# Taking part of the exponential off ScalarE: one score tile of six, in three of seven steps, computed by GpSimd and VectorE

## The chip, the cores and the metric

The kernel runs on one core of a Trainium2 chip. The metric is the device time of one execution in microseconds (us). Before the change it is 322.8 us (322.55 to 322.87 in the runs taken beside the changed kernel). All runs compared below are fast unless a run is called slow, which here means that it took over 1.5% longer than the fastest of its kernel. In the profiles, PE is TensorE's matmul, PEld its weight load, ACT ScalarE, DVE VectorE, POOL GpSimd, SP SyncE; "L280" is a line of that run's own source, so the same statement has another number before and after: the tanh is L271 before and L280 (in two runs L282) after, the exp L275 and L284, the scores' matmul L262 and L271, the pass of pv L292 and L322 (L321).

## The reference

Attention with a tanh soft cap, then a soft mixture of experts on its result. Only the first half matters here:

```python
scores = scale * np.matmul(q, k.transpose(0, 1, 3, 2))   # 8 batches, 12 heads, 448 x 448, head size 64
scores = cap * np.tanh(scores / cap)                      # cap = 30
attn = np.exp(scores - scores.max(-1, keepdims=True))
attn = attn / (attn.sum(-1, keepdims=True) + 1e-09)
x = np.matmul(attn, v)                                    # then x goes through _moe_ref(x, phi, w1, w2)
```

q and k are drawn with a deviation of 0.1, so the scores lie near 0. The kernel leaves the maximum out.

## The kernel before

A "step" handles one chunk j of six score tiles of 128 x 448 elements. ScalarE applies two tanh (three tiles each, out of PSUM) and one exp (six tiles, in SBUF). TensorE makes the scores of the next chunk and multiplies the chunk before by V (a pass of pv); VectorE normalises pv, casts k and q, and copies transposes. Seven steps make a period, one small exp of router logits (E) ends it.

```python
def tanh_chunk(i):
    j, half = divmod(i, CH // CS)                # CH = 6 tiles a chunk, CS = 3 tiles a tanh
    if half == 0:
        exs[j] = exps.tile([P, CH, S], BF16, name="ex", tag="ex")      # a ring of four
    ...
        act.activation(exs[j][:, half * CS + u0:half * CS + u1, :],
                       sc[:, u0:u1, 0:S], ACT.Tanh, scale=qk_scale / cap)

def exp_part(j, u0, u1):
    act.activation(exs[j][:, u0:u1, :], exs[j][:, u0:u1, :], ACT.Exp, scale=cap)

for j in range(NCH):                             # NCH = 56 steps (simplified: first and last ones cut)
    run(j, "0")
    tanh_chunk(2 * j)
    tanh_chunk(2 * j + 1)
    exp_chunk(j - 1)                             # exp_part(j - 1, 0, CH)
    pv_pass(pr, 0)                               # matmuls of a pass, then VectorE's normalisation
    run(j, "a")                                  # run(): casts, transposes, logits placed in the slot
    qk_chunk(2 * j + 2)
    run(j, "b")
    pv_pass(pr, 1)
    run(j, "c")
    qk_chunk(2 * j + 3)
    run(j, "d")
...
for n, job in enumerate(wjobs):                  # loads of the experts' weights
    at(2 + n * (NCH - 6) // len(wjobs), "b", *job)
```

Everything is issued in this order, in the timelines each engine runs its instructions in it (TensorE's weight loads apart; in the changed kernel VectorE stands for GpSimd ahead of L306 in 14 of 21 cases, 17.1 us in all, and nothing behind it goes first), and pv and the transposes have one PSUM buffer each.

The softmax here doesn't subtract the row's maximum and nothing guards it: scores larger than these inputs give would overflow.

Of the kernel before, what the change touches and what calls it, by code (L numbers as in the profile page):

```python
# [1 line left out]

# [5 lines left out]

F32 = mybir.dt.float32
BF16 = mybir.dt.bfloat16  # L10
ALU = mybir.AluOpType
ACT = mybir.ActivationFunctionType
PSUM = bass.MemoryType.PSUM

P = 128
# [3 lines left out]
S = 448  # L19
CH = 6  # L20
# [2 lines left out]
GOFF = (0, 128, 256, 320)  # L23
VW = 2 * (DH + 1)
MASKED = -30000.0


@with_exitstack
def kernel(
# [14 lines left out]
    E = moe_w1.shape[0]  # L44
# [5 lines left out]
    cap = float(cap)  # L50
# [4 lines left out]
    NPAIR = 2 * NQ  # L55
    NTILE = NPAIR * NT
    NCH = NTILE // CH
    R2 = 28

    ctx.enter_context(tc.manual_schedule())  # L60
    pe, dve, act, pool, sp = nc.tensor, nc.vector, nc.scalar, nc.gpsimd, nc.sync
# [5 lines left out]

    ones = consts.tile([P, P], BF16, name="ones")
    dve.memset(ones, 1.0)
    ident = consts.tile([P, P], BF16, name="ident")  # L70
    make_identity(nc, ident)
    ones32 = consts.tile([P, 1], BF16, name="ones32")
    pool.memset(ones32, 0.0)
    pool.memset(ones32[0:NS, :], 1.0)
    mask = consts.tile([P, NG, NS], F32, name="mask")
    pool.memset(mask, 0.0)
    pool.memset(mask[0:HP, NG - 1, :], MASKED)
    phib = consts.tile([P, NJ, NS], BF16, name="phib")
    ET4 = consts.tile([P, B // 2 - 1, NT, 2, HP], BF16, name="ET4")
    winv = consts.tile([P, B // 2, NT], F32, name="winv")  # L80
    slT = consts.tile([P, NJ, NS], BF16, name="slT")
    zacc = consts.tile([P, 1], F32, name="zacc")
# [4 lines left out]
           for e in range(E - 1)]  # L87
    w2b = wts.tile([P, R2, D], BF16, name="w2b")

# [17 lines left out]
    def load_half(dst, n0, half):  # L107
# [4 lines left out]
    wjobs = [(load_w1, e, jh, fh) for e in range(E) for jh in range(2) for fh in range(2)]  # L112
    wjobs += [(load_half, w2b[:, n0:n0 + 4, half * HD:(half + 1) * HD], n0, half)
              for n0 in range(0, R2, 4) for half in range(2)]

    dram = ctx.enter_context(tc.tile_pool(name="dram", bufs=1, space=bass.MemoryType.DRAM))
    w2d = []
    for n0 in range(R2, len(blocks), 4):
        t = dram.tile([P, 2, 4, HD], BF16, name=f"w2d{n0}")
        for half in range(2):  # L120
            wjobs.append((load_half, t[:, half, :, :], n0, half))
        w2d.append(t)

    att = ExitStack()
# [5 lines left out]
    exps = att.enter_context(tc.tile_pool(name="exps", bufs=4))  # L130
    vb.append(att.enter_context(tc.tile_pool(name="vb1", bufs=1)))
    xs = att.enter_context(tc.tile_pool(name="xs", bufs=4))
    attp = ExitStack()
    psS = attp.enter_context(tc.tile_pool(name="psS", bufs=2, space=PSUM))
    psV = attp.enter_context(tc.tile_pool(name="psV", bufs=1, space=PSUM))
# [115 lines left out]
    scores, exs, pvs, xq, xTs, lgs = {}, {}, {}, {}, {}, {}  # L251

    def qk_chunk(i):
        sc = psS.tile([P, CS, 512], F32, name="sc", tag="sc")
        scores[i] = sc
        for u in range(CS):
            pr, c = divmod(i * CS + u, NT)
            Q, h = divmod(pr, 2)
            r = slice(h * HP, h * HP + HP)
            for n in range(2):  # L260
                cs = slice(n * HP, n * HP + HP)
                pe.matmul(sc[cs, u, 0:S], qkT["k", Q][r, c, cs],  # L262
                          qkT["q", Q][r, :, cs], start=True, stop=True)

    def tanh_chunk(i):
        j, half = divmod(i, CH // CS)
        if half == 0:
            exs[j] = exps.tile([P, CH, S], BF16, name="ex", tag="ex")
        sc = scores.pop(i)
        for u0, u1 in ((0, 1), (1, CS)) if i == 0 else ((0, CS),):  # L270
# [4 lines that stand above are left out]
        act.activation(exs[j][:, u0:u1, :], exs[j][:, u0:u1, :], ACT.Exp, scale=cap)  # L275

    def exp_chunk(j):
        exp_part(j, 0, CH)

    def pv_tiles(pr, half, c0, c1, home=None):  # L280

# [16 lines left out]
    def norm(pr, half):  # L298
# [7 lines left out]
            pv[:, :, :, 0:DH],  # L306
            rec.to_broadcast([P, 2, 2, DH]), op=ALU.mult)

    def pv_pass(pr, half, home=None):
        pv_tiles(pr, half, 0, NT, home)  # L310
        norm(pr, half)
# [11 lines left out]
    def logits(Q, ps=None):  # L323
# [8 lines left out]
        if hq == 0:  # L332
            lgs[b] = xs.tile([P, NG, NS], F32, name="lg", tag="lg", bufs=2)
        dve.tensor_tensor(lgs[b], ps, mask if hq == 0 else lgs[b], op=ALU.add)  # L334

# [13 lines left out]
    def e_norm(b):  # L349
# [6 lines left out]
        else:  # L356
            dve.tensor_tensor(zacc, ps, zacc, op=ALU.add)
        if b == B - 1:
# [27 lines left out]
    def slot_sums(b):  # L386
# [4 lines left out]
        else:  # L391
            dve.tensor_tensor(slacc, ps, slacc, op=ALU.add)  # L392
        for hq in range(NQB):
# [8 lines left out]
    def at(j, slot, f, *a):  # L402
        if j < 0:
            j, slot = 0, "b"
        aux.setdefault((j, slot), []).append((f, a))
# [8 lines left out]
    def quad_in(Q, cast_k, cast_q, k_in, q_in, v_in):  # L414
        if 0 < Q < NQ:
            at(*cast_k, cast, "k", Q)
            at(*cast_q, cast, "q", Q)
            at(*k_in, transp, "k", Q)
            at(*q_in, transp, "q", Q)
            at(*v_in, vcast, Q)  # L420

    for b in range(B):
        j = b * PER
        if b == 0:
            quad_in(1, (0, "a"), (0, "b"), (0, "d"), (1, "a"), (2, "d"))
        else:
            quad_in(3 * b + 1, (j - 1, "b"), (j, "a"), (j - 1, "d"), (j, "c"), (j + 1, "d"))
        quad_in(3 * b + 2, (j + 1, "c"), (j + 2, "c"), (j + 2, "b"), (j + 2, "d"),
                (j + 4, "d"))
        quad_in(3 * b + 3, (j + 4, "a"), (j + 5, "a"), (j + 4, "d"), (j + 5, "c"),  # L430
                (j + 6, "d"))
        p = 6 * b
        at(j + 1, "d", spare, 26 if b == 0 else 10)
        at(j + 2, "d" if b == 0 else "a", spare, 14)
        at(j + 2, "d" if b == 0 else "c", spare, 8)
        at(j + 3, "d", spare, 10)
        at(j + 4, "a", x_transp, p)
        at(j + 5, "a", x_transp, p + 1)
        at(j + 6, "a", x_transp, p + 2)
        at(j + 5, "d", logits, 3 * b)  # L440
        if b < B - 1:
            at(j + 7, "a", x_transp, p + 3)
            at(j + 8, "a", x_transp, p + 4)
            at(j + 7, "d", logits, 3 * b + 1)
            at(j + 9, "a", x_transp, p + 5)
            at(j + 9, "d", logits, 3 * b + 2)
            at(j + 11, "0", e_exp, b)
            at(j + 11, "d", slot_sums, b)
            if b < B - 2:
                at(j + 12, "d", e_transp, b)  # L450
            if b < B - 2:
                at(j + 13, "d", e_norm, b)
            if b % 2:
                at(j + 14, "d", e_sums, b // 2)
    for n, job in enumerate(wjobs):
        at(2 + n * (NCH - 6) // len(wjobs), "b", *job)
    for j, slot, n in ((0, "a", 10), (0, "c", 10), (1, "b", 10), (1, "c", 8)):
        at(j, slot, spare, n)
    for j, slot, n in ((NCH - 6, "d", 8), (NCH - 4, "d", 8), (NCH - 2, "d", 12)):
# [5 lines left out]
    def run(j, slot):  # L465
        for f, a in aux.pop((j, slot), []):
            f(*a)
# [20 lines left out]
    def pair_at(j):  # L488

        pr = (j + 1) * CH // NT - 1  # L490
        return pr if pr >= 0 and (pr + 1) * NT > j * CH else None

    for j in range(NCH):
        run(j, "0")
        tanh_chunk(2 * j)
        if j == NCH - 1:
            exp_chunk(j - 1)
        tanh_chunk(2 * j + 1)
        if j < 2:
            exp_chunk(j)  # L500
        elif 2 < j < NCH - 1:
            exp_chunk(j - 1)
        pr = pair_at(j - 2)
        if pr is not None:
            pv_pass(pr, 0)
        run(j, "a")
        if j == NCH - 1:
            pv_pass(pr, 1)
            busy(8, psT.tile([P, P], F32, name="filler", tag="T"))
            e_norm(B - 2)  # L510
            busy(6, psT.tile([P, P], F32, name="filler", tag="T"))
            break
        qk_chunk(2 * j + 2)
        run(j, "b")
        if pr is not None:
            pv_pass(pr, 1)
        run(j, "c")
        qk_chunk(2 * j + 3)
        run(j, "d")
    assert not aux, aux.keys()  # L520
# [44 lines left out]
    for s, gs in enumerate(halves):  # L565
        hs = slice(2 * s, 2 * s + 2)
        ps = bank([P, 2, NS], name="lpl")
        for g in gs:
# [3 lines left out]
                      start=False, stop=True)  # L572
        dve.tensor_tensor(lg[:, hs, :], ps, lg[:, hs, :], op=ALU.add)
        act.activation(el[:, hs, :], lg[:, hs, :], ACT.Exp)
# [3 lines left out]
    for s in range(2):  # L578
        js = slice(3 * s, 3 * s + 3)
        dve.tensor_tensor(slT[:, js, :], sl_ps[:, js, :], slacc[:, js, :], op=ALU.add)  # L580
    e_rep(bl)
# [9 lines left out]
    for half in range(2):  # L591
        for n0 in range(R2, len(blocks), 4):
            t = tl.tile([P, 4, HD], BF16, name=f"w2t{n0}_{half}")
            sp.dma_start(out=t, in_=w2d[(n0 - R2) // 4][:, half, :, :])
            w2t[n0, half] = t
# [3 lines left out]
    def w2_half(n, half):  # L599
        if n < R2:  # L600
            return w2b[:, n, half * HD:(half + 1) * HD]
        return w2t[n - n % 4, half][:, n % 4, :]
# [90 lines left out]
    for n in range(B // 2 * NT):  # L693
        bb, c = divmod(n, NT)
# [61 lines left out]
```

## Time and profile before

| | before |
|---|---|
| time, us | 322.8 |
| span of the profiled run, us | 321.0 |
| mean granted TensorE clock | 0.983 |
| busy, us: ScalarE / TensorE / VectorE / GpSimd | 284.4 / 273.3 / 168.6 / 104.5 |
| from one E to the next (seven steps), us | 32.92 |

The last row is (255.78 - 58.23) / 6 from the starts of E in ScalarE's timeline. The lines that carry this page, and the timeline of one group of steps, are in the prediction. One more view: the busy windows of the kernel before for three steps, with the columns start:end, length, busy us (and instruction count) of PE, PEld, DVE, ACT and POOL, granted clock, DMA share and GB/s.

```profile
77.13:81.80 4.67, 4.51 (x69) 3.30 (x67) 2.84 (x7) 4.67 (x4) 1.10 (x2) 1.00 1.16 230
81.80:86.48 4.68, 3.55 (x52) 2.44 (x50) 2.03 (x5) 4.68 (x5) 3.28 (x4) 1.00 0.77 216
86.48:91.15 4.67, 4.16 (x57) 3.04 (x57) 1.84 (x5) 4.67 (x4) 0.00 (x0) 1.00 1.15 216
```

ScalarE is busy the whole of each step, TensorE at 76 to 97% of it (3.55/4.68 to 4.51/4.67), and the clock is full. Of TensorE's 12.22 us in these three steps, 3.0 are junk matmuls, which are issued whether it is late or not.

### The profile page before, as it was taken

The page shows a single profiled execution, that of the slowest core. Times are in us where ns is not written, and L with a number is a line of the kernel's source. Part 1 is how long each engine was busy: PE and PEld are TensorE (multiplying, and loading weights), DVE is VectorE, ACT ScalarE, POOL GpSimd, SP SyncE. Part 2 cuts the span into 40 slices and gives each one's busy share as a digit, 9 for nine tenths or more (in the row PEclk, how much of TensorE's full clock was granted, in tenths as well). Part 3 has the DMA queues.
Part 4 walks back from the last instruction along what each step waited for, and adds up shares of the span by engine and source line. Part 5 has one row for each costly group of instructions (what it writes and reads, how often), then busy time and mean ns, then how long its engine had stood idle before and what let it go on. Part 6 is the DMA issues. An engine that isn't in the chain of part 4 may idle for free.

```text
span 321.0 us, 8842 instructions
## 1 busy us (share of the span) xinstructions
PE 273.3 (85%) x3827; PEld 193.6 (60%) x3827; DVE 168.6 (53%) x427; ACT 284.4 (89%) x208; POOL 104.5 (33%) x133
## 2 busy tenths in 40 slices
PE   8889988899889988898889988988889998998720
PEld 6666666666656666665666656766666667652300
DVE  3545664465546654665466546644665434327740
ACT  4998999999999999999999999999999999226730
POOL 2063525433533452445154515451643030200000
PEclk9999999999999999999999999999999999999985
DMA  8689999999999989999999999999999816678996
GB/s 240 226 178 228 225 274 238 220 229 261 220 209 251 254 197 233 238 279 240 200 231 266 227 227 218 265 225 224 224 258 201 207 51 208 225 308 307 378 414 278
DMA packets 57623, 76.91 MB, mean 240 GB/s; under 512 B 3824, under 2 KB 54128, under 8 KB 57584
## 3 DMA queue, kind: packets, MB, share of 16 engines
q0 software_dynamic: 30480, 25.22, 52.0%
q1 hardware_dynamic: 26816, 50.90, 46.5%
q8 instruction: 30, 0.49, 0.6%
q10 hardware_dynamic: 288, 0.23, 0.2%
q14 instruction: 9, 0.07, 0.1%
HBM read 90.54 MB, written 18.09 MB: 338 GB/s over the span
## 4 chain that ended last, share of the span: by engine, by line
ACT 77%; PE 13%; DVE 2%; DMA 2%; issue 2%; DVEq 0%; SPq 0%; ACTq 0%
ACT ex L271 38%; ACT ex L275 37%; PE so_ps L638 2%; PE hp L612 2%; DMA out_dram<-ob 2%; PE pv L292 1%; PE op L664 1%; PE boot L476 1%; PE junk L476 1%; PE sc L262 1%; DMA out_dram<-obh 1%; PE ps L189 1%; ACT ob L716 1%; DVE obh L666 1%; DVE xq L303 1%
## 5 line engine op out<-in xcount | busy, mean ns | idle before, releaser
L271 ACT ACTIVATE ex<-sc 128x1344 bf16<-128x1344 f32 (+1 forms) x113 | 162.4, 1693 | 2.3 <-PE pv L292 1.4
L275 ACT ACTIVATE ex<-ex 128x2688 bf16<-128x2688 bf16 (+1 forms) x57 | 161.9, 2858 | 0.1
L292 PE MATMUL pv<-vbd,ex 128*128 128x130 bf16 x1288 | 90.3, 220 | 2.1 <-ACT ex L275 0.7
L292 PEld LDWEIGHTS <-ex 128*128 128x128 bf16 x1344 | 78.8, 97 | 21.0 <-DVE xq L303 14.7
L262 PE MATMUL sc<-qT,kT 64*64 64x448 bf16 x672 | 78.7, 358 | 10.7 <-ACT ex L271 10.2
L240 POOL CAST vbd<-vraw 64x896 bf16<-64x896 f32 x23 | 21.6, 941 | 106.6 <-PE pv L292 76.2
L302 DVE RECIPROCAL rec<-pv 128x4 f32<-128x4 f32 x92 | 16.8, 183 | 60.4 <-PE pv L292 60.4
L262 PEld LDWEIGHTS <-kT 64*64 64x64 bf16 x672 | 28.0, 105 | 27.8 <-issue 10.0
L303 DVE TENSOR_TENSOR xq<-pv,rec 128x256 bf16<-128x256 f32 x92 | 39.0, 424 | 3.2
L476 PEld LDWEIGHTS <-ones 128*128 128x128 bf16 x497 | 30.4, 101 | 12.4 <-DVE xq L303 8.6
L476 PE MATMUL junk<-ones 128*128 128x128 bf16 x454 | 33.0, 219 | 2.8 <-DVE xq L303 1.9
L346 POOL COPY e<-E 128x512 bf16<-128x512 bf16 x9 | 5.5, 608 | 85.2 <-ACT E L340 49.6
L232 DVE COPY kT<-kps 128x896 bf16<-128x896 bf16 x23 | 14.4, 625 | 28.0 <-PE kps L230 28.0
L105 POOL DMA_DIRECT2D w1b<-in_moe_w_dram x32 | 24.8, 779 | 0.0
L241 POOL CAST vbd<-vraw 64x896 bf16<-64x896 f32 x23 | 23.6, 1027 | 1.3
L320 DVE COPY xT<-xps 128x512 bf16<-128x512 bf16 x47 | 19.5, 415 | 3.2 <-PE xps L318 3.2
L318 PE MATMUL xps<-ident,xq 128*128 128x128 bf16 x188 | 18.1, 218 | 0.0
L219 DVE CAST kbf<-kraw 128x896 bf16<-128x896 f32 x22 | 16.9, 767 | 0.8 <-DMA kraw<-in_k_dram 0.8
L232 DVE COPY qT<-qps 128x896 bf16<-128x896 bf16 x23 | 14.2, 618 | 4.5 <-PE qps L230 4.5
L230 PE MATMUL kps<-ident,kbf 128*128 128x128 bf16 x161 | 12.8, 219 | 4.2 <-DVE slacc L392 2.2
L230 PE MATMUL qps<-ident,qbf 128*128 128x128 bf16 x161 | 12.8, 219 | 3.2 <-DVE lg L334 2.7
L230 PEld LDWEIGHTS <-kbf 128*128 128x128 bf16 x161 | 10.0, 97 | 9.0 <-issue 8.3
(103 smaller groups left out, 229.5 us busy)
## 6 DMA issues: line engine op xcount, KB each, us to landing
w1b<-in_moe_w_dram POOLq DMA_DIRECT2D x32, 384.0 KB, 9.0
vraw<-in_v_dram SPq DMA_DIRECT2D x23, 448.0 KB, 5.3
qraw<-in_q_dram SPq DMA_DIRECT2D x22, 448.0 KB, 7.8
kraw<-in_k_dram SPq DMA_DIRECT2D x22, 448.0 KB, 5.3
w2d<-in_moe_w_dram POOLq DMA_DIRECT2D x18, 384.0 KB, 9.2
w2t<-w2d SPq DMA_DIRECT2D x18, 384.0 KB, 5.0
w2b<-in_moe_w_dram POOLq DMA_DIRECT2D x14, 384.0 KB, 9.2
out_dram<-ob SPq DMA_DIRECT2D x7, 768.0 KB, 7.6
```

The source lines that it names most:

```text
L105: pool.dma_start(out=w1b[e][:, js, fs], in_=w1r[:, e, js, fs])
L230: pe.transpose(ps[:, c, :], src[:, c, :], ident)
L232: dve.tensor_copy(t, ps)
L240: pool.tensor_copy(t[0:HP, :, :, 0:DH], raw[0:HP])
L241: pool.tensor_copy(t[HP:P, :, :, DH + 1:VW - 1], raw[HP:P])
L262: pe.matmul(sc[cs, u, 0:S], qkT["k", Q][r, c, cs], qkT["q", Q][r, :, cs], start=True, stop=True)
L271: act.activation(exs[j][:, half * CS + u0:half * CS + u1, :], sc[:, u0:u1, 0:S], ACT.Tanh, scale=qk_scale / cap)
L275: act.activation(exs[j][:, u0:u1, :], exs[j][:, u0:u1, :], ACT.Exp, scale=cap)
L292: pe.matmul(pvs[pr, half][:, n, 0:VW], exs[j][:, u, GOFF[g]:GOFF[g] + P], vbds[Q % 2][:, h, c, :], start=(c == 0 and n == 0), stop=(c == N ...
L303: dve.tensor_tensor(xq[Q][:, 2 * half:2 * half + 2, h * P:(h + 1) * P] .rearrange("p g (i d) -> p g i d", i=2), pv[:, :, :, 0:DH], rec.to_ ...
L320: dve.tensor_copy(t, ps)
L476: pe.matmul(junk if home is None else home, ones, ones, start=True, stop=True)
```

## The change

Its intent: ScalarE is the bound, so in three of seven steps its exp takes five tiles instead of six. The sixth tile's exp(cap * t) is 2^n * 2^r: GpSimd scales, rounds to n by adding and subtracting 1.5 * 2^23, and builds the bits of the power of two; VectorE takes the rest r and evaluates a polynomial of degree 4 in five operations. V casts move one or more steps later, and 24 instead of 28 weight blocks stay resident, which frees SBUF for the three new tiles.

```diff
-    R2 = 28
+    R2 = 24
-            wjobs.append((load_half, t[:, half, :, :], n0, half))
+            wjobs.insert(4 * E + 2 * len(w2d) + half, (load_half, t[:, half, :, :], n0, half))
+    xe, xr, xp = (xs.tile([P, S], dt, name=nm, tag=nm, bufs=1)
+                  for nm, dt in (("xe", I32), ("xr", F32), ("xp", F32)))
-        exp_part(j, 0, CH)
+        exp_part(j, 1 if j in shared else 0, CH)
+    shared = [j for j in range(4, NCH - 2) if (j + 1) % 7 in (1, 2, 3)] if cap < 80 else []
+    def split_exp(j):
+        t, c = exs[j][:, 0, :], cap * math.log2(math.e)
+        pool.tensor_scalar(xr, t, c, ROUND, ALU.mult, ALU.add)
+        pool.tensor_scalar(xr, xr, -ROUND, None, ALU.add)
+        pool.tensor_scalar(xe, xr, POW2[0], 2.0 ** 23, ALU.add, ALU.mult)
+    def poly_exp(j, part):
+        if part == 0:
+            dve.scalar_tensor_tensor(xr, exs[j][:, 0, :], cap * math.log2(math.e), xr, ALU.mult, ALU.subtract)
+            dve.scalar_tensor_tensor(xp, xr, POW2[1], xr, ALU.add, ALU.mult)
+            dve.scalar_tensor_tensor(xp, xp, POW2[2], xr, ALU.add, ALU.mult)
+        else:
+            dve.scalar_tensor_tensor(xp, xp, POW2[3], xr, ALU.add, ALU.mult)
+            dve.scalar_tensor_tensor(exs[j][:, 0, :], xp, POW2[4], xe.bitcast(F32), ALU.add, ALU.mult)
     ... (V casts: slots (j + 1, "d"), (j + 4, "d"), (j + 6, "d") become (j + 2, "c"), (j + 5, "c"), (j + 7, "c"))
-        at(2 + n * (NCH - 6) // len(wjobs), "b", *job)
+        at(1 + n * (NCH - 3) // len(wjobs), "b", *job)
         run(j, "a")
+        if j - 1 in shared:
+            poly_exp(j - 1, 0)
         qk_chunk(2 * j + 2)
         run(j, "b")
+        if j in shared:
+            split_exp(j)
         pv_pass(pr, 1)
         run(j, "c")
+        if j - 1 in shared:
+            poly_exp(j - 1, 1)
         qk_chunk(2 * j + 3)
```

More of the change, by code (lines that the diff above doesn't have):

```diff
@@ L1 @@
+import math
 from contextlib import ExitStack
@@ L10 @@
 BF16 = mybir.dt.bfloat16
+I32 = mybir.dt.int32
 ALU = mybir.AluOpType
@@ L25 @@
 MASKED = -30000.0
+POW2 = (120.232421875, 5.80956259, 24.9511916, 71.9877637, 103.860479)
+ROUND = 1.5 * 2.0 ** 23
 @with_exitstack
@@ L277, in exp_chunk @@
     def exp_chunk(j):
-        exp_part(j, 0, CH)
+        exp_part(j, 1 if j in shared else 0, CH)
[7 more added lines that the diff above has]
+        if part == 0:
+            dve.scalar_tensor_tensor(xr, exs[j][:, 0, :], cap * math.log2(math.e), xr,
+                                     ALU.mult, ALU.subtract)
+            dve.scalar_tensor_tensor(xp, xr, POW2[1], xr, ALU.add, ALU.mult)
+            dve.scalar_tensor_tensor(xp, xp, POW2[2], xr, ALU.add, ALU.mult)
+        else:
+            dve.scalar_tensor_tensor(xp, xp, POW2[3], xr, ALU.add, ALU.mult)
+            dve.scalar_tensor_tensor(exs[j][:, 0, :], xp, POW2[4], xe.bitcast(F32),
+                                     ALU.add, ALU.mult)
     def pv_tiles(pr, half, c0, c1, home=None):
@@ L426 @@
         else:
-            quad_in(3 * b + 1, (j - 1, "b"), (j, "a"), (j - 1, "d"), (j, "c"), (j + 1, "d"))
+            quad_in(3 * b + 1, (j - 1, "b"), (j, "a"), (j - 1, "d"), (j, "c"), (j + 2, "c"))
         quad_in(3 * b + 2, (j + 1, "c"), (j + 2, "c"), (j + 2, "b"), (j + 2, "d"),
-                (j + 4, "d"))
+                (j + 5, "c"))
         quad_in(3 * b + 3, (j + 4, "a"), (j + 5, "a"), (j + 4, "d"), (j + 5, "c"),
-                (j + 6, "d"))
+                (j + 7, "c"))
         p = 6 * b
```

## The prediction

> **What bounds the kernel now.** I read the page first: busy shares, the chain that ended last, the costliest groups.
>
> ```profile
> span 321.0 us, 8842 instructions
> ...
> PE 273.3 (85%) x3827; PEld 193.6 (60%) x3827; DVE 168.6 (53%) x427; ACT 284.4 (89%) x208; POOL 104.5 (33%) x133
> ...
> ACT  4998999999999999999999999999999999226730
> ...
> ACT 77%; PE 13%; DVE 2%; DMA 2%; issue 2%; DVEq 0%; SPq 0%; ACTq 0%
> ...
> L271 ACT ACTIVATE ex<-sc 128x1344 bf16<-128x1344 f32 (+1 forms) x113 | 162.4, 1693 | 2.3 <-PE pv L292 1.4
> L275 ACT ACTIVATE ex<-ex 128x2688 bf16<-128x2688 bf16 (+1 forms) x57 | 161.9, 2858 | 0.1
> ```
>
> ScalarE is the bound in the attention stage: saturated from slice 2 to 34, 77% of the chain, and its tanh and exp groups waited 2.3 and 0.1 us in all. Its records overlap (mean 2858 ns for an exp), so I take distances between starts instead. The timeline of ScalarE and then of VectorE in the stretch where the change acts:
>
> ```profile
> 77.13 2.65 ACT L271 ACTIVATE ex<-sc 128x1344 bf16<-128x1344 f32 x2
> 79.47 2.64 ACT L275 ACTIVATE ex<-ex 128x2688 bf16<-128x2688 bf16 x1
> 81.80 2.67 ACT L271 ACTIVATE ex<-sc 128x1344 bf16<-128x1344 f32 x2
> ```
>
> Two tanh take 79.47-77.13 = 2.34 us and one exp 81.80-79.47 = 2.33 us, so a step is 4.67 us. Counting back from the small exp of step 11 at 58.23 us, 77.13 starts step 15; 14, 15, 16 are the shared steps of the third group.
>
> ```profile
> 78.93 0.41 DVE L320 COPY xT<-xps 128x512 bf16<-128x512 bf16 x1
> 80.16 0.18 DVE L302 RECIPROCAL rec<-pv 128x4 f32<-128x4 f32 x1 [0.81 <-PE pv L292]
> 80.38 0.42 DVE L303 TENSOR_TENSOR xq<-pv,rec 128x256 bf16<-128x256 f32 x1
> 80.72 1.33 DVE L219 CAST kbf<-kraw 128x896 bf16<-128x896 f32 x1
> ...
> 85.18 0.62 DVE L219 CAST qbf<-qraw 128x896 bf16<-128x896 f32 x1
> 86.06 0.29 DVE L334 TENSOR_TENSOR lg<-lps,lg 128x128 f32<-128x128 f32 x1 [0.27 <-PE lps L329]
> ```
>
> VectorE is 53% busy on average, but TensorE follows it closely: after the add into lg, TensorE transposes q into the bank just freed, then starts the next pass of pv and only then the scores for ScalarE:
>
> ```profile
> 86.41 0.55 PE L230 MATMUL qps<-ident,qbf 128*128 128x128 bf16 x7 [0.38 <-DVE lg L334]
> 86.80 0.97 PE L292 MATMUL pv<-vbd,ex 128*128 128x130 bf16 x14
> 88.04 0.76 PE L262 MATMUL sc<-qT,kT 64*64 64x448 bf16 x6 [0.28 <-ACT ex L271]
> ```
>
> These scores end at 88.80 and ScalarE wants them at 91.35. So this path, through the single buffers for transposes and for pv, has about 2.5 us of slack. Last I read the busy windows: in the steps beginning at 77.13, 81.80 and 86.48 VectorE is busy 2.84, 2.03 and 1.84 us.
>
> [...] No operation of two SBUF inputs is in this trace, but the qbf cast, [...] took 0.62 us[...]. [...] the kbf cast at 80.72 took 1.33 instead of 0.62 us beside a GpSimd V cast from 80.64 to 81.56. [...]
>
> **The change part by part.** *Removed:* 448 of 2688 elements in 21 exps (steps 7, 8, 9 to 49, 50, 51): [...] 0.373 us each, 7.84 us in all, 1.12 per period of seven steps. All of it lies on the bound; alone it would give 322.84-7.84 = 315.0, faster by 2.4%.
>
> *Added on GpSimd:* three tensor_scalar of 448 per shared step. From its casts (896 elements 0.94, 512 elements 0.61 us) 448 is 0.55 us, an estimate, 0.6 with the wait on the one before: 1.8 us a tile. GpSimd is 33% busy; it has the time.
>
> *Added on VectorE:* five operations on fp32, each waiting on the one before. 0.62 us plus 0.03 (the gap between reciprocal and multiply above) is 0.65: 1.95 for the first three, 1.3 for the last two, 3.25 a tile, 68 us in all. In steps 15 to 17 VectorE's demand goes from 6.71 us (6.0 without the cast's block) to 15.8, and ScalarE would give it 3 x 4.30 = 12.9. This decides.
>
> *The order of the waits:* the changed source issues split_exp(j) before the last two operations for j-1, and there is one xr, xe, xp. So GpSimd's next split starts when the third operation of j-1 is done, and the fourth waits for that split. (It thereby reads the next tile's rounded part, a flaw of value in two of three tiles; the scores of this data are near 0, so I expect the result to pass.) VectorE is strictly in order, so its normalisation, casts and copies stand behind.
>
> By hand, in us from the start of step 15: xT copied 2.2; three operations for 14 to 4.15; normalisation to 4.8; the kbf cast behind GpSimd's first split operation 4.8 to 5.4; second and third split operation to 6.0 and 6.6; fourth and fifth operation to 7.9; xT to 8.3; three for 15 to 10.25; kT to 10.85; the qbf cast, again behind GpSimd, to 11.5; split of 16 to 12.7; last two for 15 to 14.0; lg 14.3; transposes of q 14.95; pass of pv 15.9; scores 16.7. ScalarE wants them at 12.9, so it stands 3.8 us. The next scores stand behind a pv pass that waits for a normalisation, about 0.6 more; by the third step VectorE has caught up. Together 4.4 lost against 1.12 gained: 3.3 a period, seven periods 23 us: 346.
>
> *Moved:* the V casts now stand behind the splits, needed only two steps on: nothing. *Residency:* 20 instead of 18 reloads of weights, 1.9 us apart (32.13 us for 18 in the queue's timeline); the last was issued at 280.1, and its weights were used about 293: 0 to 1 us.
>
> **The rivals.** (a) No waits on GpSimd [...]: the same chain with VectorE alone is 7.9 us of arithmetic and norm, copies and casts to lg at 11.9, scores at 14.3: 1.4 lost, then some 0.6 and 0.2, net 1.1 to 1.2 a period, about 331. For it: the split is partly beside the normalisation and cast. Against it: 4.15 to 4.8 and 5.4 are too short to hold 1.8 us. (b) All hidden: 315. It needs VectorE's operations near 0.5 us and free of waits; the casts' 0.62 us speaks against it. [...] (d) TensorE becomes the bound by itself: in these three steps 12.2 us of its busy time include 3.0 us of junk matmuls, so no.
>
> **Range and chances.** Between the hand schedule (346) and (a) (331), with the size of each block unknown, I take 338. Low 322: operations of 0.5 to 0.55 us with half of the stall gone. High 362: [...] slower GpSimd operations. Faster by over 2% needs ScalarE to lose less than about 0.2 us a period: 0.06. Within 2% (below 329.3): 0.2. Slower: 0.74.
>
> **What would show it.** Right: the ScalarE tanh group waits tens of us on TensorE, mostly once in seven steps, at the tanh two steps after the group's last shared step; ScalarE's busy time falls although the span grows; VectorE's group for the fourth operation idles on GpSimd; steps outside the shared ones keep 4.67 us. Each VectorE operation about 0.62 us, each GpSimd one about 0.55. Wrong: VectorE operations well under 0.6 us, or ScalarE still without gaps, which would leave 315; or time gained or lost after 275 us, in the tail.

## The result, and the profile after

| | before | changed |
|---|---|---|
| time, us (median of 4) | 322.80 | 379.44 (377.35 to 382.04) |
| ratio, 95% interval | | 1.176 (1.1665 to 1.1856) |
| span, us; mean granted clock | 321.0; 0.983 | 375.6; 0.894 |
| busy, us: ScalarE / TensorE / VectorE / GpSimd | 284.4 / 273.3 / 168.6 / 104.5 | 280.7 / 293.4 / 228.9 / 169.5 |
| E to E, us | 32.92 | 40.77 |

All ratios in this document are the mean time of one kernel's fast runs over that of the other's fast runs in the same rounds, so they are not quite the ratio of the medians. The changed kernel's result passes the comparison with the reference, as forecast.

The last number is (304.58 - 59.97) / 6; single periods take 39.6 to 41.9 us. Seven periods that are 40.77 - 32.92 = 7.85 us longer make 55 of the 56.6 us. The page of the changed kernel, against the lines of the prediction:

```profile
PE 293.4 (78%) x3827; PEld 207.5 (55%) x3827; DVE 228.9 (61%) x532; ACT 280.7 (75%) x208; POOL 169.5 (45%) x196
...
PEclk9999996999599975998589978997599969999995
...
PE 51%; DVE 19%; POOL 12%; ACT 7%; DMA 5%; issue 3%; DVEq 0%; POOLq 0%; ACTq 0%; SPq 0%
...
L280 ACT ACTIVATE ex<-sc 128x1344 bf16<-128x1344 f32 (+1 forms) x113 | 140.4, 1288 | 51.0 <-PE pv L322 37.7
...
L296 POOL TENSOR_SCALAR xr<-xr 128x448 f32<-128x448 f32 x21 | 31.8, 1514 | 1.7
...
L306 DVE SCALAR_TENSOR_TENSOR xp<-xp,xr 128x448 f32<-128x448 f32 x21 | 13.1, 622 | 17.1 <-POOL xr L296 17.1
```

ScalarE's busy time fell a little, but its tanh group now stands idle for 51.0 us, and it makes 7% of the chain that ended last instead of 77%. TensorE takes its place with 51%, with VectorE and GpSimd behind it. (ScalarE's busy sum fell by less than the saving, probably because its records overlap differently when it waits: an exp of six tiles averages 2880 ns in the records before and 2454 after. Distances between starts are the safe measure.) Three things stand out that the prediction did not have: GpSimd's second operation takes 1514 ns, the granted clock sinks to 5 to 9 tenths about once a period, and TensorE is busy for 20 us more with the same 3827 matmuls. The fourth VectorE operation (L306) did wait for GpSimd, as forecast.

Now one group of three shared steps. The timeline of the changed kernel, cut to the lines of the argument; columns are start, length, engine, line, operation, tile, and in brackets the idle time before and who ended it:

```profile
130.16 1.59 POOL L296 TENSOR_SCALAR xr<-xr 128x448 f32<-128x448 f32 x1
...
131.78 0.62 DVE L306 SCALAR_TENSOR_TENSOR xp<-xp,xr 128x448 f32<-128x448 f32 x1 [1.22 <-POOL xr L296]
...
135.59 1.29 ACT L280 ACTIVATE ex<-sc 128x1344 bf16<-128x1344 f32 x1 [1.91 <-PE sc L271]
...
139.72 0.28 DVE L364 TENSOR_TENSOR lg<-lps,lg 128x128 f32<-128x128 f32 x1
140.06 0.91 PE L239 MATMUL qps<-ident,qbf 128*128 128x128 bf16 x7 [3.43 <-DVE lg L364]
140.09 0.31 ACT L370 ACTIVATE E<-lg 128x128 bf16<-128x128 f32 x1 [1.25 <-DVE lg L364]
...
140.75 1.73 PE L322 MATMUL pv<-vbd,ex 128*128 128x130 bf16 x14
...
142.41 1.33 PE L271 MATMUL sc<-qT,kT 64*64 64x448 bf16 x6
...
145.19 1.29 ACT L280 ACTIVATE ex<-sc 128x1344 bf16<-128x1344 f32 x1 [4.78 <-PE pv L322]
```

Read it from the bottom. ScalarE stands 4.78 us before its tanh, for TensorE. TensorE had stood 3.43 us before its transposes of q, for VectorE's add into lg. VectorE came to this add late because the operations of the shared tiles stand before it in its queue, and because GpSimd's 1.59 us operation held that queue for 1.22 us, and again in the next step. Something else is new: the same matmuls that took 0.55, 0.97 and 0.76 us before now take 0.91, 1.73 and 1.33. The busy windows over the same stretch give the reason in the clock column (columns as above; the last row is the stretch after the wait of 3.43 us):

```profile
123.44:127.84 4.40, 4.05 (x64) 2.94 (x65) 2.97 (x9) 4.40 (x4) 2.65 (x3) 1.00 0.55 133
127.84:132.39 4.55, 3.44 (x46) 2.31 (x44) 3.23 (x7) 4.42 (x4) 2.71 (x3) 1.00 0.92 189
132.39:135.50 3.11, 1.63 (x21) 1.09 (x21) 2.59 (x6) 1.29 (x1) 1.28 (x2) 0.99 0.65 150
135.50:140.09 4.59, 0.46 (x11) 0.48 (x10) 2.83 (x6) 3.25 (x2) 4.03 (x4) 0.50 0.43 71
140.09:145.19 5.10, 5.10 (x41) 3.91 (x40) 3.02 (x6) 0.31 (x2) 4.99 (x7) 0.50 0.49 116
```

TensorE works only 1.63 + 0.46 = 2.09 of 7.70 us, its clock falls to half, and then it is busy for all of 5.10 us with work for which it needed little more than half the time before. But look at the moment: the clock is at half from 135.4 us on, and the wait of 3.43 us begins only at 136.6. That wait did not bring the clock down, it came too late. Ahead of the fall TensorE had worked 1.63 of 3.11 us, and its longest gap was 1.52 us. Of the seven groups, four show the fall before the long wait begins, and three 0.4 to 1.6 us into it (windows of 0.5 us over the trace).

In this group ScalarE waits 1.91 + 1.25 + 4.78 = 7.9 us, and 0.83 a step later, where the prediction's working had 4.4.

### The profile page after: what moved, and what is told of

It is laid out like the page before. It is cut to its first block, busy times and chain, and to the rows that moved or that the text cites. A ratio compares the mean times of both kernels' runs of the same rounds, so it can differ in the third digit from the quotient of the medians.

```text
span 375.6 us, 9071 instructions
## 1 busy us (share of the span) xinstructions
PE 293.4 (78%) x3827; PEld 207.5 (55%) x3827; DVE 228.9 (61%) x532; ACT 280.7 (75%) x208; POOL 169.5 (45%) x196
## 4 chain that ended last, share of the span: by engine, by line
PE 51%; DVE 19%; POOL 12%; ACT 7%; DMA 5%; issue 3%; DVEq 0%; POOLq 0%; ACTq 0%; SPq 0%
PE pv L322 20%; PE sc L271 11%; POOL xr L296 6%; POOL xe L297 4%; ACT ex L280 3%; DMA kraw<-in_k_dram 3%; PE junk L506 3%; DVE xp L303 3%; PE qps L239 3%; DVE xp L304 3%; ACT ex L284 2%; DVE ex L307 2%; DVE xr L301 2%; POOL xr L295 2%; DVE xq L333 2%
## 5 line engine op out<-in xcount | busy, mean ns | idle before, releaser
L280 ACT ACTIVATE ex<-sc 128x1344 bf16<-128x1344 f32 (+1 forms) x113 | 140.4, 1288 | 51.0 <-PE pv L322 37.7
L284 ACT ACTIVATE ex<-ex 128x2688 bf16<-128x2688 bf16 (+2 forms) x57 | 129.6, 2277 | 0.1
L322 PE MATMUL pv<-vbd,ex 128*128 128x130 bf16 x1288 | 101.0, 236 | 1.9 <-ACT ex L284 0.7
L322 PEld LDWEIGHTS <-ex 128*128 128x128 bf16 x1344 | 89.4, 106 | 22.9 <-DVE xq L333 19.9
L271 PE MATMUL sc<-qT,kT 64*64 64x448 bf16 x672 | 84.4, 381 | 1.5 <-ACT ex L280 1.2
L295 POOL TENSOR_SCALAR xr<-ex 128x448 f32<-128x448 bf16 x21 | 11.7, 558 | 82.5 <-issue 42.8
L332 DVE RECIPROCAL rec<-pv 128x4 f32<-128x4 f32 x92 | 16.7, 182 | 44.2 <-PE pv L322 43.8
L239 PE MATMUL qps<-ident,qbf 128*128 128x128 bf16 x161 | 15.3, 246 | 25.4 <-DVE lg L364 24.0
L296 POOL TENSOR_SCALAR xr<-xr 128x448 f32<-128x448 f32 x21 | 31.8, 1514 | 1.7
L239 PEld LDWEIGHTS <-qbf 128*128 128x128 bf16 x161 | 11.8, 109 | 26.8 <-issue 21.2
L239 PE MATMUL kps<-ident,kbf 128*128 128x128 bf16 x161 | 12.7, 218 | 14.6 <-DVE xT L350 9.9
L306 DVE SCALAR_TENSOR_TENSOR xp<-xp,xr 128x448 f32<-128x448 f32 x21 | 13.1, 622 | 17.1 <-POOL xr L296 17.1
L241 DVE COPY kT<-kps 128x896 bf16<-128x896 bf16 x23 | 14.3, 622 | 9.8 <-PE kps L239 9.8
```

The costliest lines, as they stand in the source:

```text
L239: pe.transpose(ps[:, c, :], src[:, c, :], ident)
L271: pe.matmul(sc[cs, u, 0:S], qkT["k", Q][r, c, cs], qkT["q", Q][r, :, cs], start=True, stop=True)
L280: act.activation(exs[j][:, half * CS + u0:half * CS + u1, :], sc[:, u0:u1, 0:S], ACT.Tanh, scale=qk_scale / cap)
L295: pool.tensor_scalar(xr, t, c, ROUND, ALU.mult, ALU.add)
L296: pool.tensor_scalar(xr, xr, -ROUND, None, ALU.add)
L322: pe.matmul(pvs[pr, half][:, n, 0:VW], exs[j][:, u, GOFF[g]:GOFF[g] + P], vbds[Q % 2][:, h, c, :], start=(c == 0 and n == 0), stop=(c == N ...
```

## The experiments

The base of each diff is the changed kernel, unless another is named. The kernel before took 322.47 to 322.81 us beside these runs (medians of the rounds; single runs 322.1 to 325.1).

**1. The moved parts alone** (V casts, resident blocks, earlier weight loads; exps whole again):

```diff
-        exp_part(j, 1 if j in shared else 0, CH)
+        exp_part(j, 0, CH)
-            poly_exp(...) ; split_exp(...)      # all three calls
```

> Only the moved parts: V casts behind the next steps, 24 blocks resident, weight transfers in the new order; every exp whole on ScalarE. Theory (the loss is the chain VectorE - GpSimd - TensorE in three steps of seven): the moved parts cost nothing, 322 to 324 us. Rival (the V casts or the two more reloads carry a share of the 56.6 us): over 330.

Measured 326.73 us (324.58 to 327.84), ratio 1.0115 (1.0065 to 1.0164). The loss is at the start. In the waits of this run (engine, tile and line, what it waited for: us in total, times, longest), a cast of k at the start stands longer for its data:

```profile
DVE kbf L228 <- DMA kraw<-in_k_dram: 6.1, 1, 6.1
```

The cast ran at 19.57 us, in the kernel before at 14.62 after 0.84 us of waiting, and ScalarE's tanh group waits 6.5 us in all instead of 2.3. So "nothing" for the moved parts was wrong by 4 us. Experiment 2 tells which part.

**2. The moved parts with the weight loads at their old spacing**, from step 2:

```diff
+        exp_part(j, 0, CH)                       # as in 1
-        at(1 + n * (NCH - 3) // len(wjobs), "b", *job)
+        at(2 + n * (NCH - 6) // len(wjobs), "b", *job)
```

> The moved parts alone, whole exps (326.7 us), but the weight transfers begin at step 2 in the old spacing. Theory (the 4 us are lost in the first 30 us, where the first weight transfer overtakes the load of k): 322 to 323, as before. Rival (the V casts a step later or the two more reloads cost it): 326.

Measured 322.65 us (322.48 to 323.01), ratio 0.9988 (0.9946 to 1.0031). The 4 us are the early weight loads: with the old spacing the cast of k runs at 15.89 us instead of 19.57. The later V casts and two more reloads cost nothing that can be seen.

**3. The short exp alone**, with no split and no polynomial, so the sixth tile keeps its tanh: values wrong (relative error 0.28).

```diff
-            poly_exp(...) ; split_exp(...)      # all three calls; exp_part(j, 1, CH) stays
```

> The 21 short exps and the moved parts, but nothing in place of the missing exp (wrong values on purpose). Theory: ScalarE's saving is real and all of it reaches the end when nothing else is added: 322.8 - 7.8 = 315, ScalarE without waits in the middle. Rival (TensorE or a transfer becomes the bound as soon as a step is shorter): 318 to 323.

Measured 318.40 us (316.98 to 319.56), ratio 0.9858 (0.9808 to 0.9909). Against experiment 1 this is 8.3 us less; E to E is 31.79 us, 1.13 less than before, where the prediction had 1.12. The saving is real, and from the first period on ScalarE waits for nobody when nothing is added.

**4. VectorE's operations without GpSimd's split.** The power and the rounded part are constants (valid, as the scores are near 0), so the values stay right:

```diff
+    pool.memset(xr, 0.0)
+    pool.memset(xe.bitcast(F32), 0.00962816)
-        if j in shared:
-            split_exp(j)
```

> As changed, but GpSimd computes no split: xr and xe are set once (wrong values on purpose), VectorE does all its five operations and never waits for GpSimd. Theory (GpSimd's waits, 1.7 us twice per group, and what follows from them are most of the loss): 328 to 340, TensorE's clock stays near 0.98. Rival (VectorE's 15 operations per group alone do it): over 365.

Measured 355.82 us, ratio 1.1024 (1.0962 to 1.1086), clock 0.926, values right (the expectation calls them wrong): between the two expectations. Against experiment 3 the five operations alone cost 37.4 us. ScalarE's group in this run:

```profile
L280 ACT ACTIVATE ex<-sc 128x1344 bf16<-128x1344 f32 (+1 forms) x113 | 140.5, 1301 | 38.9 <-PE pv L322 34.0
```

The prediction's rival (a), "331 without GpSimd", is wrong by 25 us: 33.3 of the 56.6 us (355.8 - 322.5) need no split on GpSimd. GpSimd's V casts still run here, and beside them single operations of VectorE take up to 1.39 us; the five average 653 to 722 ns, against 616 to 639 ns in the changed kernel.

**5. GpSimd's split without VectorE's operations**, values wrong as in 3:

```diff
-            poly_exp(j - 1, 0)
-            poly_exp(j - 1, 1)
```

> As changed, but VectorE does none of its five operations; GpSimd computes its three per shared step (wrong values on purpose). Theory: GpSimd alone is off every path, 314 to 317, and its middle operation shows whether 1.5 us is its own cost (then it stays over 1.2 us) or a block by VectorE (then about 0.55). Rival [...]: over 322.

Measured 318.21 us, ratio 0.9859 (0.9813 to 0.9905): GpSimd's work is free by itself (318.40 in experiment 3). But its middle operation is as slow here without VectorE's five operations (1479 against 1514 ns), so the length is its own:

```profile
L296 POOL TENSOR_SCALAR xr<-xr 128x448 f32<-128x448 f32 x21 | 31.1, 1479 | 1.7
L297 POOL TENSOR_SCALAR xe<-xr 128x448 int32<-128x448 f32 x21 | 13.0, 620 | 1.7
```

The first and the third operation (L295 and L297) have two arithmetic steps and take 591 and 620 ns; the middle one has one, and takes 1479.

**6. The middle operation written with two arithmetic steps**, the second a multiplication by 1:

```diff
-        pool.tensor_scalar(xr, xr, -ROUND, None, ALU.add)
+        pool.tensor_scalar(xr, xr, -ROUND, 1.0, ALU.add, ALU.mult)
```

> As changed, but GpSimd's middle operation gets a second, empty operation (times 1.0), the form of its two neighbours. Theory (the 1.48 us is the price of this one-operation form): it falls to 0.55 to 0.65 us, each split is 0.9 us shorter, and VectorE's wait for it goes from 1.2 us to about 0.3; 379 becomes 362 to 370. Rival (the length is not its form, or its length is hidden): 376 to 382.

Measured 369.34 us, ratio 1.1451 (1.1377 to 1.1526). Its two lines:

```profile
L296 POOL TENSOR_SCALAR xr<-xr 128x448 f32<-128x448 f32 x21 | 15.6, 744 | 1.7
...
L306 DVE SCALAR_TENSOR_TENSOR xp<-xp,xr 128x448 f32<-128x448 f32 x21 | 13.1, 622 | 6.3 <-POOL xr L296 6.3
```

The form cost 10 us: half the length, and VectorE waits 6.3 instead of 17.1 us.

**7. TensorE's clock.** 50 filler matmuls ahead of the late transposes of q keep it at work while it waits:

```diff
+        if nm == "q" and Q % 3 == 2 and Q > 2:
+            spare(50)
```

> As changed, but 50 junk matmuls fill the 3.4 us in which TensorE waits for VectorE ahead of the transposes of q. They change no wait. Theory ([...] the half clock stretches the matmuls that follow by some 2.4 us a group): the granted clock stays near 0.98, and 379 becomes 360 to 366. Rival (the clock is a symptom, the path is VectorE and GpSimd alone): clock up, time 376 to 382.

Measured 367.54 us, ratio 1.1395 (1.1344 to 1.1446), clock 0.967 instead of 0.894. About 12 us of the loss were the half clock. The fillers do not prevent it everywhere: the clock still falls in three of the seven groups, and TensorE runs 14 us in all at half clock instead of 72 (estimates from windows of 0.5 us). **7b**, the same with 24 fillers on the kernel of experiment 4:

> VectorE's five operations on constants without GpSimd's split, as before (355.8 us), with 24 junk matmuls ahead of the transposes of q. Theory: this is the case of my hand schedule (331 for VectorE's queue alone, and 4 for the moved parts at the start): 333 to 342 with the clock near 0.98. Rival (VectorE's queue costs more than the hand schedule says): over 348 although the clock is full.

Measured 349.81 us, ratio 1.0845 (1.0814 to 1.0877), clock 0.957: 6 us less than experiment 4. Less than I expected, so most of VectorE's share is not the clock.

**8. Two sets of the three tiles**, which also makes all values right; 20 resident blocks to make room:

```diff
-    R2 = 24
+    R2 = 20
+    xsets = [[xs.tile(...) for xe, xr, xp] for n in range(2)]
+        xe, xr, xp = xsets[j % 2]               # in split_exp and in poly_exp
```

> As changed, but two sets of xe, xr and xp in turn (right values in all tiles) and 20 blocks resident to make room; no split waits for VectorE and VectorE does not wait for the next split. Theory (GpSimd's length is then off the path): about as without the split, 350 to 358. Rival [...]: over 370.

Measured 360.83 us in the fast run (366.46 in one called slow), against 377.35 for the fastest run of the changed kernel: 16.5 us less without the shared set (the two kernels differ in the resident blocks too). This lies between the two expectations; VectorE's operations are longer here, 668 to 826 ns. Only one fast run, so no interval.

**9. A fifth buffer in the ring of exp tiles**, on the kernel of 7b, because the tanh seemed to wait for the pv pass that frees the oldest:

```diff
+    exps = att.enter_context(tc.tile_pool(name="exps", bufs=5))     # and R2 = 20
```

> The run without the split and with junk matmuls (349.8 us), with five score buffers in turn instead of four (20 blocks resident to make room). In it ScalarE's first tanh two steps after the group stands 2.1 to 3.9 us for the second pass of pv, the last reader of the buffer that it overwrites. Theory (that reader is a wait of its own, beyond the scores): the tanh then waits for its scores only, 1.2 to 1.5 us less a group, 338 to 342. Rival (the scores come no earlier than that pass in effect): 348 to 351.

Measured 352.41 us, ratio 1.0911 (1.085 to 1.0973): no gain. The wait only changes its name, from the pv pass to the scores.

**10. VectorE's operations at half width**, on the kernel of experiment 4. The five operations work on 224 of 448 columns; the others stay tanh values, so the result is wrong (relative error 0.14):

```diff
-            dve.scalar_tensor_tensor(xp, xr, POW2[1], xr, ALU.add, ALU.mult)
+            dve.scalar_tensor_tensor(xp[:, 0:S // 2], xr[:, 0:S // 2], POW2[1], xr[:, 0:S // 2], ALU.add, ALU.mult)
             ... (all five alike)
```

> VectorE's five operations alone (no GpSimd split, constants as the power and the rest), as in a3_no_split (355.8), but on 224 of the tile's 448 columns; the other 224 keep what ScalarE's short exp leaves uninitialised or old, so values are wrong on purpose if they are not covered. If the loss follows the length of VectorE's queue, the five operations cost 5 x 0.3 = 1.6 us less a tile and some 2 us less ahead of the scores: 325 to 333. If it is a fixed cost of each instruction or of the order in which they stand, over 345.

Measured 325.09 us in the fast run, clock 0.980 (331.88 in one called slow). One fast run, no interval, but 30 us is far outside any spread here. One of the five operations at half width and, in the second fence, in experiment 4 (busy us of 21 and mean ns):

```profile
L306 DVE SCALAR_TENSOR_TENSOR xp<-xp,xr 128x224 f32<-128x224 f32 x21 | 10.6, 505 | 0.0
```

```profile
L306 DVE SCALAR_TENSOR_TENSOR xp<-xp,xr 128x448 f32<-128x448 f32 x21 | 14.4, 685 | 0.0
```

The other four go from 15.2, 15.0, 14.3 and 13.7 to 10.1, 10.4, 9.5 and 9.0 us, so the sums are 72.6 and 49.6 us: 23 us less on VectorE and 30 us less in time. The 6 us of half clock (7b) are also gone, as the clock is 0.98; 23 + 6 is about the whole. But the first 49.6 us on VectorE cost only 325.1 - 318.4 = 6.7 us (against experiment 3), and the next 23 cost 30.7. So the length of VectorE's queue is what counts, and not in proportion: a part of it fits into TensorE's lead, and what goes beyond is lost almost whole. The trace of this run also shows the lead wear off: no wait of ScalarE is listed in the first two periods, and 0.4 to 1.6 us in each of the five after.

**11. All repairs together**: experiments 6, 7 and 8 and the weight loads of experiment 2 in one kernel.

> All repairs together, right values: two sets of the split's tiles, the two-operation form on GpSimd, 50 filler matmuls that keep TensorE's clock, weights loaded from step 2 on. If the parts of the loss add up, what is left is that of VectorE's operations with a full clock: b2_warm_no_split's 349.8 less 4 for the start, about 345. If GpSimd still holds up VectorE, over 355.

Measured 352.52 us, ratio 1.0918 (1.0871 to 1.0965), clock 0.972, ScalarE's tanh group idle 31.0 us. This is between the two expectations: the repairs take 27 us off, but not to 345. VectorE's operations took 625 to 867 ns a group here instead of 0.62, and its timeline shows what ran beside them: 0.61 to 0.63 us with GpSimd idle or issuing transfers (57 of 105), up to 0.92 beside its tensor_scalar and up to 1.37 beside its casts.

**12. One tile in seven steps instead of three**, last tile of chunk 1 of a period, split at the end of step 1, first part of the polynomial in step 2, second at the end of step 3, the two-step form, weight loads as in experiment 2:

```diff
+    shared = [j for j in range(4, NCH - 4) if j % 7 in (1,)] if cap < 80 else []
+        exp_part(j, 0, CH - 1 if j in shared else CH)
+        if (j - 1) % 7 == 1 and j - 1 in shared:
+            poly_exp(j - 1, 0)                  # after run(j, "a")
+        if (j - 2) % 7 == 1 and j - 2 in shared:
+            poly_exp(j - 2, 1)                  # after run(j, "d"), with split_exp(j)
```

> One tile in seven steps only (chunks 1, 8, ...), its last tile instead of its first so that it is needed a step later; VectorE's first three operations fill its gap in the step without pv, the last two stand at the end of the next step; GpSimd's middle operation in the two-operation form, the split after the last reader of its tiles (right values), weights from step 2. Theory (what counts is whether the five operations meet a gap of VectorE): ScalarE stands nowhere, 7 x 0.373 = 2.6 us gained, 320 to 321. Rival (any 3.25 us on VectorE shift TensorE): 323 or more.

Measured 326.08 us (323.77 to 327.31), ratio 1.0088 (1.0032 to 1.0144): missed. Its timeline in one such step:

```profile
116.03 0.94 POOL L249 CAST vbd<-vraw 64x896 bf16<-64x896 f32 x1
116.04 1.43 DVE L303 SCALAR_TENSOR_TENSOR xp<-xr 128x448 f32<-128x448 f32 x1
...
117.03 1.25 POOL L250 CAST vbd<-vraw 64x896 bf16<-64x896 f32 x1
...
117.50 1.25 DVE L304 SCALAR_TENSOR_TENSOR xp<-xp,xr 128x448 f32<-128x448 f32 x1
...
119.34 0.35 PE L359 MATMUL lps<-phib,xT 128*128 128x32 bf16 x8 [1.38 <-DVE kT L241]
...
120.46 1.64 PE L322 MATMUL pv<-vbd,ex 128*128 128x130 bf16 x14
```

VectorE's operations take 1.43 and 1.25 us beside GpSimd's V casts, the copy of kT comes late, TensorE stands 1.38 us, and its next pass of pv runs at half speed (1.64 instead of 0.97 us, granted clock 0.50). The theory held for two periods: the first two from E to E take 32.56 and 32.55 us, without a wait of ScalarE; the later ones take 33.6 to 34.7.

**13. Two tiles in seven steps**, chunks 1 and 3, placed in the same way.

> As the run with one tile, and a second tile in seven steps (chunks 3, 10, ...), first three operations at the end of the next step, last two at the end of the step after. Theory: 14 x 0.373 = 5.2 us gained if both meet gaps: 317 to 319. Rival (VectorE then lacks the gap at the third or fourth step, TensorE's passes slip): 321 or more.

Measured 365.71 us (362.19 to 367.33), ratio 1.1309 (1.123 to 1.1387), clock 0.891. Missed by nearly 50 us. Two tiles placed badly cost almost as much as the whole change with three.

**14. One tile in seven steps, where GpSimd is idle.** As experiment 12, but the last tile of chunk 2, split at the end of step 2, the polynomial's first two operations after the first normalisation of step 3 and three at its end:

```diff
-    shared = [j for j in range(4, NCH - 4) if j % 7 in (1,)] if cap < 80 else []
+    shared = [j for j in range(4, NCH - 2) if j % 7 == 2] if cap < 80 else []
+        if j - 1 in shared:
+            poly_exp(j - 1, 0)                  # two operations, after run(j, "a")
+        if j - 1 in shared:
+            poly_exp(j - 1, 1)                  # three operations, after run(j, "d")
+        if j in shared:
+            split_exp(j)                        # after run(j, "d")
```

> One tile in seven steps, split and polynomial placed in steps 2 and 3 where GpSimd casts and issues nothing. The saving is one tile's 0.373 us in each of 7 periods, 2.6 us: 319.9 against c1_start's 322.5 if ScalarE never waits for it. If the VectorE operations still delay a transposed tile by more than TensorE's lead, 322 or more.

Measured 320.15 us (319.75 to 320.35), ratio 0.9913 (0.9887 to 0.9939), values right. Its page:

```profile
PE 273.2 (86%) x3827; PEld 193.6 (61%) x3827; DVE 189.5 (60%) x462; ACT 281.7 (88%) x208; POOL 118.2 (37%) x154
...
ACT 76%; PE 12%; DMA 3%; issue 3%; DVE 2%; DVEq 0%; ACTq 0%; SPq 0%
...
L280 ACT ACTIVATE ex<-sc 128x1344 bf16<-128x1344 f32 (+1 forms) x113 | 162.7, 1699 | 2.2 <-PE pv L321 1.4
```

ScalarE is the bound again, with 2.2 us of waiting in all, and E to E is 32.54 us, 0.38 less than before. This is the same idea at a third of its size, and it beats both kernels, if only by 0.9%, inside the 2% that count as the same. Between experiments 12 and 14 two things changed together, the place in VectorE's queue and what GpSimd does beside it; no run parts them.

**15. A second tile three steps later** (chunk 5), where GpSimd is idle too but VectorE is busy for 2.9 of 4.7 us:

```diff
-    shared = [j for j in range(4, NCH - 2) if j % 7 == 2] if cap < 80 else []
+    shared = [j for j in range(4, NCH - 2) if j % 7 in (2, 5)] if cap < 80 else []
```

> A second tile, three steps after the first of v3_one_step3: its split stands at the end of step 5 and its polynomial in step 6, where the trace of v3_one_step3 shows GpSimd without work (0.00 and 0.37 us busy in two steps) but VectorE busy for 2.9 of the step's 4.7 us. Two tiles save 2 x 0.373 x 7 = 5.2 us: 317.3 if ScalarE never waits. If it is the length of VectorE's queue in a few neighbouring steps that counts (2.9 + 3.1 is more than a step), the scores come late, TensorE falls behind, and it takes over 321.

Measured 341.82 and 344.41 us in the fast runs (two more, called slow, at about 350), ratio 1.0631 (1.0589 to 1.0672). Two of its waits:

```profile
PE pv L321 <- DVE xq L332: 12.6, 8, 2.8
...
DVE xr L302 <- POOL xe L297: 5.6, 5, 2.2
```

TensorE's passes of pv wait for VectorE's normalisation, behind the polynomial. That speaks for the queue of VectorE, as expected; but in five periods the split also came late and held VectorE for 5.6 us, so this run does not part the two causes cleanly.

## Why the prediction was wrong

The direction and the mechanism were right: slower, the stall at the tanh two steps after the group's last shared step, the chain through VectorE's queue, lg, the transposes of q and pv, and the fourth operation waiting for the next split. The time was not: 338 forecast, 346 in the hand schedule, at most 362, and 379.4 measured. The hand schedule was made for step 15, in the second group. Here it is against the trace, in us from the start of the group's first step: step 8 (45.32 us), before which there are no shared steps, step 15 (83.66 us) and step 22 (123.44 us).

| event | by hand | step 8 | step 15 | step 22 |
|---|---|---|---|---|
| xT copied | 2.2 | 2.1 | 3.35 | 4.0 |
| three operations done | 4.15 | 3.9 | 5.2 | 5.9 |
| k cast done | 5.4 | 5.2 | 6.4 | 7.1 |
| second, third split operation done | 6.0, 6.6 | 6.4, 7.4 | 7.6, 8.7 | 8.3, 9.4 |
| fifth operation done | 7.9 | 8.1 | 9.4 | 10.0 |
| split of the next tile done | 12.7 | 13.75 | 15.0 | 15.7 |
| last two operations done | 14.0 | 14.4 | 15.7 | 16.4 |
| lg | 14.3 | 14.6 | 15.9 | 16.6 |
| transposes of q, pv pass, scores done | 14.95, 15.9, 16.7 | 15.6, 17.1, 18.35 | 16.8, 18.35, 19.6 | 17.5, 19.0, 20.3 |
| tanh starts | (from 16.7) | 19.2 | 21.1 | 21.75 |

The failing step is the sum that gave "4.4 lost against 1.12 gained: 3.3 a period", and its use for all seven periods. Measured, ScalarE waits 5.7 us in the first group and 7.6 to 8.8 us in each of the other six, and a period is 7.85 us longer. The terms of the sum, with what each measured:

1. *The starting point was taken from the kernel before, for every group.* In the first group that is right: xT comes at 2.1 us, and VectorE's work up to lg stays within about 0.4 us of the schedule. In step 15 xT is 1.1 us late (3.35 against 2.21 in the same step of the kernel before), ahead of any shared operation on VectorE in the group, and in step 22 1.25 us (4.0 against 2.76 there; in every second period a small reciprocal, winv, stands before it). All that follows is late by the same time. So TensorE does not regain its lead in the four plain steps between two groups. The six later groups cost 8.2 us on average against 5.7 in the first: about 2.5 us each, 15 in all, an estimate from this one trace. The wearing off in experiments 10 and 12 fits it; no run changed it alone.
2. *The wait for GpSimd's middle operation.* "0.55 us, an estimate, 0.6 with the wait" was right for the first operation (558 ns) and wrong for the middle one (1514 ns) and the third (875 ns). The estimate came from casts, which have another form. In the first group this hardly shows, by chance: the schedule also let the second split operation wait 0.6 us for the k cast, and it did not wait (it starts at 4.8 us). Experiment 6 puts the middle operation at 10 us of the total, experiment 8 the whole hold through the one set of tiles at 16.5 us; they overlap.
3. *The half clock was not in the sum.* In the last row but one, step 22, the three TensorE pieces take 0.91 + 1.73 + 1.33 = 3.97 us where 0.55 + 0.97 + 0.76 = 2.28 were assumed. This trace shows the granted clock fall to 0.50, and not after one long idle time: as said above, it came after thin work with gaps of at most 1.52 us, before or early in the wait of 3.43 us. Experiment 7 prices it at 12 us. A forecast that holds TensorE up for some us should have asked at once what becomes of its clock.
4. *The slack was counted to the scores only.* The tanh also waited for the second pass of pv, the last reader of the buffer that it overwrites; it starts 0.9 to 1.45 us after the scores. Experiment 9 shows that one more buffer alone gains nothing.
5. *"Moved: nothing"* was 4 us (experiments 1 and 2), and the cause is the earlier start of the weight loads, a line of the diff that I had passed over. The rest of the moved parts was nothing, as forecast.
6. *Rival (a), 331 without GpSimd*, measured 355.8. VectorE's operations without a split are most of the loss: experiment 10 shows that it depends on the length of VectorE's queue.

One slip changed nothing: 14, 15 and 16 are the shared steps of the second group, not of the third.

In sums: the start +4 (1 and 2), the saving -8.3 (3 against 1), VectorE's operations +37.4 (4 against 3), GpSimd's split beside them 379.4 - 355.8 = +23.6, together 56.7 of 56.6. These are differences of successive kernels, so they must add up; the parts inside them (clock 12, form 10, shared set 16.5) overlap and must not be added.

What held: the saving (7.84 us forecast, 8.3 measured; the 0.373 us of a tile was an estimate, and in the changed kernel an exp of 2240 elements takes 2079 ns and one of 2688 takes 2454, 375 ns more); the length of VectorE's operations (0.62 us forecast, after the cast of q; 616 to 639 ns). Rival (d) was right that TensorE's work alone is no bound: with filler matmuls added, experiment 7 got faster (367.54 against 379.44 us).

## What to carry to other kernels

Moving work off the bound to an engine that is "53% busy" is judged by the queue in which it will stand, and by how much lead the engines after it have, not by its share: here TensorE, 87% busy in the steps shown (12.22 of 14.02 us), could not make good what VectorE's queue had cost it. Ask of each new delay what it does to TensorE's clock: here it fell to half (0.50) after 3.11 us in which TensorE had worked 1.63. Look at the first period and at a later one apart: here the first lost 5.7 us and the later ones 8.2 on average. If an offload fails, try a third of it in the step where GpSimd has nothing else to do: one tile in seven gained 0.9%, where three lost 17.6%.

## What the runs measured of the engines

- GpSimd's tensor_scalar with one arithmetic step in fp32: 1479 to 1514 ns for 128 x 448, against 558 to 875 ns for the forms with two (means in the changed kernel and experiments 5 and 6).
- VectorE's scalar_tensor_tensor on 448 elements: the fp32 forms took 622 to 639 ns, the form with one bf16 source 616 ns (means in the changed kernel).
- TensorE's granted clock: in experiment 12 it fell to half (0.50) with no single gap above 1.38 us in the stretch ahead, only thin work (0.83 us busy of 2.35 in the busy windows, then a pass of pv of 1.64 instead of 0.97 us), and in the changed kernel after 1.63 us busy of 3.11. A reader who watches for long gaps alone will miss it.
- Beside GpSimd's casts VectorE's two-input operations took up to 1.65 us (experiment 12, at 217.56 us), beside its DMA issues alone 0.61 to 0.63 us in all 27 cases of the changed kernel's timeline. One case in experiment 12, of 1.20 us beside two DMA issues, stays unexplained.
